# An attention and mixture-of-experts kernel: three buffers for x, and the last pair's first two groups stored later

## The chip, the cores and the metric

One core of one Trainium2 chip runs the whole program. The number that counts is the device time of one execution in microseconds (us); the median of three executions stands for the kernel. Lower is better.

The engines are named as in the profile: PE (TensorE, matmuls), DVE (VectorE), ACT (ScalarE), POOL (GpSimd) and SP (SyncE, which here does nothing but issue transfers and read expert numbers). Each works through its own list of instructions in order. The lists meet at semaphores.

## The reference

Windowed attention on 8 batches, 8 heads, 576 positions, 64 channels; half of the heads see the last 32 positions, half see every fourth of the last 128. Its output, as 4608 rows of 512, goes through a mixture of experts with 4 groups of 4 experts: each row picks a group, then an expert in the group, and gets that expert's two-layer result times the two probabilities.

```python
scores = np.where(mask, scale * q @ k.T, -1e9)
x = softmax(scores) @ v                       # 4608 rows of 512
g_idx = argmax(x @ w_group); e_idx = argmax(x @ w_expert[g_idx])
h  = np.maximum(x[rows] @ w1[g, e], 0.0)
out[rows] = g_w * e_w * (h @ w2[g, e])
```

## The kernel before

**Attention.** The program runs 36 steps (`NT`), `NJ` = 9 to a pair of batches; a step covers 64 positions of both batches of the pair. Three steps make a group `g` (12 groups), the unit of the transfers: q, k and v are loaded by group, and the output x of three steps lies in one tile `xg[g]`, which has two buffers (line 369). The loop over `s` (line 950) is skewed: in turn `s` it computes the scores of step `s`, transposes the probabilities of step `s-1`, multiplies step `s-2` with v (`av`), writes its x (`normalise`, line 371, on DVE) and transposes the x of step `s-3`.

**Stores of x.** `store_x(g, bbs)` writes the rows of one batch (`bbs` = 0 or 1) of a group to the table `xd` in DRAM, in four or five transfers of the SP queue (lines 346, 351 and 358). They are issued in `normalise`: batch 0 when the third step of the group is written, batch 1 one turn later. Group 11, the last, is stored behind the loop (line 1009). The last pair is groups 9, 10 and 11. A tile x of group `g` may be written again only when the stores of the group before in the same buffer have landed.

**Routing.** When a pair is through, `route` computes which expert each of its rows goes to, in small pieces between the steps (`slot`). One of its pieces builds, on POOL, a mask `okm` (line 510) and from it two halves of the table `mv` (line 513); PE multiplies both with `ohl` into `tb_ps` (line 553), from which DVE updates the table of rows per expert (lines 562 to 567). The probabilities go to `xd` too (`gt`, line 547).

**The experts that start early.** After the second and the third pair the two fullest experts so far are picked (`pick`), their first rows are fetched from `xd` (`fetch_rows`, on POOL, tile `xe`), and their feed-forward work (`early`) runs among the last steps of attention and behind it, in the order that the string `TAIL` spells. Then come all other experts, one after the other, up to the end.

**Weights.** `load_weights` brings an expert's weights in 8 chunks (0 to 7) of 512 KB (line 645, SP queue), through four staging buffers `w`. ACT writes the high half of a chunk as float16 (line 667); the low half, the chunk less its high half, is made by DVE (line 663) or, for the chunks in `ASIDE`, by POOL in two instructions (line 660 scales the chunk in place, line 661 subtracts). For the first early expert these are all chunks but chunk 6. A staging buffer is free for the chunk four further on when its low half is done. The first expert's chunks are spread over turns 27 and on, one a turn (`prefetch`, `WSTEPS`, line 1003).

**Who sets the order.** PE's and DVE's lists are in the order of the code in this part of the program (line 949), so are SP's and ACT's (line 141). POOL's list is arranged by the scheduler that builds the program, which means that a change of the code elsewhere can rearrange it. Within a list nothing overtakes. An SP transfer also waits until the one eight places before it has landed.

Of the kernel before, what the change touches and what calls it, by code (L numbers as in the profile page):

```python
# [8 lines left out]
F32 = mybir.dt.float32  # L9
F16 = mybir.dt.float16  # L10
BF16 = mybir.dt.bfloat16
I32 = mybir.dt.int32
# [5 lines left out]
P = 128  # L18
# [5 lines left out]
NE = 16  # L24
NBP = B // 2
NJ = S // 64
NT = NBP * NJ
# [12 lines left out]
MAXOV = 64  # L40
# [4 lines left out]
EARLY_STEPS = {NT - 1: 1, NT: 2, NT + 1: 1}  # L45
TAIL = "ararrrarrawrrrawrwarrrrrrwbwarbrrrwbrrrrwbrrrwbTwbbb"
ASIDE = ((0, 1, 2, 3, 4, 5, 7), (4, 5, 6))
NR = NE + NEARLY
REG = 8192
NCHK = NTOK // P  # L50
# [6 lines left out]
def moe_attention_kernel(ctx, tc, q, k, k0, v, cmask, wgate, wpack, out):  # L57
    nc = tc.nc
    pool = lambda name, bufs=1, **kw: ctx.enter_context(tc.tile_pool(name=name, bufs=bufs, **kw))
    cp = pool("cp")  # L60
# [130 lines left out]
        nc.vector.memset(capt[:, r : r + 1], float(CAPS[r]))  # L191
    top = cp.tile([P, NEARLY, NE], F32, name="top")
    topc = cp.tile([P, NEARLY], F32, name="topc")
    perm = cp.tile([P, NE, NE], F32, name="perm")
    ordf = cp.tile([P, NE], F32, name="ordf")
    ordi = cp.tile([P, NE], I32, name="ordi")
    ovn = cp.tile([P, 1], I32, name="ovn")
    ovt = cp.tile([P, MAXOV, 2], I32, name="ovt")
    E16 = [cp.tile([P, TPB + 1, 4, 4], BF16, name=f"E16{i}") for i in range(2)]
    for t in E16:  # L200
        nc.vector.memset(t, 0.0)
# [15 lines left out]
    ap = apool("ap", 3)  # L217

    def run(gens, n=1):
        got = None  # L220
        for _ in range(n):
            while gens:
                try:
                    got = next(gens[0])
                    break
                except StopIteration:
                    gens.pop(0)
            else:
                return None
        return got  # L230
# [107 lines left out]
    xg = {}  # L338

    def store_x(g, bbs):  # L340
        bp, k = g // 3, g % 3
        for bb in bbs:
            row = (2 * bp + bb) * S
            xv = xg[g].rearrange("p j (h c) -> p j h c", h=2)
            own = xd[row + 192 * k : row + 192 * k + 192, :].rearrange("(j i) d -> i j d", i=64)
            nc.sync.dma_start(own[:, :, 0:256], xv[64 * bb : 64 * bb + 64, :, 0])
            for i0, i1, j0, j1, t0 in class_runs(k):
                for_all = xd[row : row + S, 256:512].rearrange("(t r) d -> r t d", r=4)[t0 % 4]
                first, n = t0 // 4, i1 - i0
                if j1 - j0 == 1:  # L350
                    nc.sync.dma_start(for_all[first : first + n], xv[64 * bb + i0 : 64 * bb + i1, j0, 1])
                    continue
                at = bass.AP(
                    for_all.tensor,
                    for_all.offset + first * 4 * XW,
                    [[4 * XW, n], [256 * XW, j1 - j0], [1, 256]],
                )
                nc.sync.dma_start(at, xv[64 * bb + i0 : 64 * bb + i1, j0:j1, 1])

    def normalise(n):  # L360
        o = oo.pop(n)
        ov = o[:, :, 0:260].rearrange("p k (s c) -> p k s c", c=65)
        den = ap.tile([P, 2, 4], F32, name="den")
        nc.vector.tensor_scalar_add(den, ov[:, :, :, 64], 1e-9 / SX)
        slot()
        nc.vector.reciprocal(den, den)
        slot()
        if n % 3 == 0:
            xg[n // 3] = ap.tile([P, 3, 512], F32, name="x", bufs=2)
        x = xg[n // 3][:, n % 3]  # L370
        nc.vector.tensor_tensor(
            x.rearrange("p (k s c) -> p k s c", k=2, s=4),
            ov[:, :, :, 0:64],
            den.unsqueeze(3).broadcast_to([P, 2, 4, 64]),
            ALU.mult,
        )
        if n % 3 == 2:
            if n < NT - 1:
                store_x(n // 3, (0,))
        elif n % 3 == 0 and n:  # L380
            store_x(n // 3 - 1, (1,))
        st[n] = x.rearrange("p (s w c) -> p s w c", s=4, w=2)

# [222 lines left out]
    def order():  # L606
        T = lambda nm, shape, dt=F32: sm.tile([P] + shape, dt, name=nm)
        key = T("key", [NE])
        nc.vector.tensor_tensor(key, base[NBP], base[0], ALU.subtract)
        for r in range(NEARLY):  # L610
            nc.vector.scalar_tensor_tensor(
                key, top[:, r], float((NEARLY - r) * NTOK), key, ALU.mult, ALU.add
            )
        nc.vector.scalar_tensor_tensor(key, key, float(NE), iota[:, 0:NE], ALU.mult, ALU.subtract)
        sq = T("sq", [NE, NE])
        nc.vector.tensor_tensor(
            sq,
            key.unsqueeze(1).broadcast_to([P, NE, NE]),
            key.unsqueeze(2).broadcast_to([P, NE, NE]),
            ALU.is_gt,  # L620
        )
        rank = T("rank", [NE])
        nc.vector.tensor_reduce(rank, sq, axis=AX.X, op=ALU.add)
        nc.vector.tensor_tensor(
            perm,
            rank.unsqueeze(1).broadcast_to([P, NE, NE]),
            iota[:, 0:NE].unsqueeze(2).broadcast_to([P, NE, NE]),
            ALU.is_equal,
        )
        nc.vector.tensor_tensor(sq, perm, iota[:, 0:NE].unsqueeze(1).broadcast_to([P, NE, NE]), ALU.mult)  # L630
        nc.vector.tensor_reduce(ordf, sq, axis=AX.X, op=ALU.add)
        nc.vector.tensor_copy(ordi[:, NEARLY:NE], ordf[:, NEARLY:NE])
# [282 lines left out]
    def prefetch():  # L915
        for r in range(NEARLY):
            while r not in ev:
                yield
            todo.extend(load_weights(ev[r], wsets[r], lambda i: i in ASIDE[r], 2 - 2 * r))
            todo.pop(0)()  # L920
# [29 lines left out]
    for s in range(NT + 3):  # L950
        ripe = bool(gate)
        if s < NT:
            scores(s)
        if s % 3 == 2 and s // 3 + 2 < NT // 3:
            load_k(s // 3 + 2, (0,))
        if s % 3 == 0 and 2 <= s // 3 + 1 < NT // 3:
            load_k(s // 3 + 1, (1,))
        if s % 3 == 1 and 1 <= s // 3 + 1 < NT // 3:
            carry_k(s // 3 + 1)
        if s % 3 == 0 and NQ <= s // 3 + 2 < NG:  # L960
            load_q(s // 3 + 2) if s // 3 + 2 < NG - 1 else None
        if s // 3 + 2 == NG - 1:
            load_q(NG - 1, s % 3, s % 3 + 1)
        if 0 <= s - 2 < NT:
            av(s - 2)
            if ripe:
                gate.clear()
        if start:
            n = start[0]
            routes.append(route(n, turned_logits(n)))  # L970
            rate[0] = RATE[n]
        if 0 <= s - 1 < NT:
            transpose_p(s - 1)
        if s < NT:
            softexp(s)
        if s == 0:
            nc.vector.memset(flat(vt[2]), 0.0)
        if 0 <= s - 3 < NT:
            transpose_x(s - 3)
        if s % 3 == 1 and 2 <= s // 3 + 2 < NG - 1:  # L980
            load_v(s // 3 + 2)
        if s // 3 + 1 == NG - 1 and s % 3 < 2:
            load_v(NG - 1, ((0, 2), (2, 3))[s % 3])
        if 0 <= s - 2 < NT:
            normalise(s - 2)
        if start:
            n = start.pop()
        if gate == [3]:
            gate.clear()
        slot()  # L990
        if s % 3 == 0 and s // 3 + 1 < NT // 3:
            shift_v(s // 3 + 1, 0, 2)
        if s % 3 == 1 and s // 3 + 1 < NT // 3:
            shift_v(s // 3 + 1, 2, 3)
        for r in picked:
            if r not in ev:
                expert(r)
        if s == min(WSTEPS):
            wq.append(prefetch())
        if s == NT - 1:  # L1000
            eb.append(early(0, new_x(fe, EARLY[0]), fe, EARLY[0]))
        run(eb, EARLY_STEPS.get(s, 0))
        run(wq, WSTEPS.get(s, 1))
        if s >= 3 and (s - 3) % NJ == NJ - 1:
            bp = (s - 3) // NJ
            if bp < NBP - 1:
                start.append(bp)
        run(eq)
# [6 lines left out]
    fh = pool("fh", 2, reuse_waits="tile")  # L1015
    rows = pool("rows", 2, reuse_waits="tile")
    fs = pool("fs", 3, reuse_waits="tile")
    wB[:] = [fs.tile([P, 4096], F16, name=nm, bufs=1) for nm in ("wb1h", "wb1l", "wb2h", "wb2l")]
    big = pool("big", reuse_waits="tile")
    stages.append(pool("wst2", reuse_waits="tile"))  # L1020

    def overflow():
# [16 lines left out]
        )  # L1039
        num = T("num", [NR])  # L1040
        nc.vector.tensor_reduce(num[:, 0:NE], cg, axis=AX.X, op=ALU.add)
# [4 lines left out]
        yield  # L1046
        cum = T("cum", [NR])
        nc.vector.tensor_copy(cum, num)
        for r in range(1, NR):
            nc.vector.tensor_tensor(cum[:, r : r + 1], cum[:, r : r + 1], cum[:, r - 1 : r], ALU.add)  # L1050
            if r % 4 == 0:
                yield
        nc.vector.tensor_copy(ovn, cum[:, NR - 1 : NR])
        lo = T("lo", [NR])
        nc.vector.tensor_tensor(lo, cum, num, ALU.subtract)
        ex = T("ex", [NR])
        nc.vector.tensor_copy(ex[:, 0:NE], ordf)
# [60 lines left out]
    run(wq, 100)  # L1118
    cur = begin(0)
    order()  # L1120
    expert(2)
    run(e1, 100)
# [128 lines left out]
```

## Time and profile before

| | |
|---|---|
| median of 3 executions | 559.17 us (558.96 to 560.13) |
| the profiled execution | 565.16 us |
| its span, first to last instruction | 563.4 us |
| PE busy | 537.1 us, 95% of the span |
| DVE, ACT, POOL busy | 369.9, 316.3, 241.1 us |
| transfers | 134.31 MB, mean 238 GB/s |

Times in the rows count from the start of the profiled span. The last scores are issued at 136.3 us, so attention takes about the first quarter and the experts the rest. The engine whose busy share matters most is PE; a busy PE counts matmuls that overlap, so its 95% says that there are few gaps, not that each matmul runs at its best.

### The profile page before, as it was taken

To read this page: it belongs to the slowest core of one execution; us is meant where nothing else is said; L and a number is where in the kernel's file an instruction comes from. 1 tells how busy PE (TensorE), PEld (TensorE's weight loads), DVE (VectorE), ACT (ScalarE), POOL (GpSimd) and SP (SyncE) were. 2 spreads that over 40 slices of the span, in tenths; PEclk is the share of its full clock that TensorE was granted. 3 is DMA by queue.
4 is the path that set the end of the run, shared out by engine and by line. 5 is a ranking of instruction groups with operands and counts; after the bars stand their busy time and mean duration, and the time that the engine had idled before them with its cause. 6 is when DMAs were issued, how large, how long until landed. Compare 5 with 4: busy or idle time off the path is not lost. (4 is left out here: it accounts for less than half of the span.)

```text
span 563.4 us, 16475 instructions
## 1 busy us (share of the span) xinstructions
PE 537.1 (95%) x6577; PEld 384.8 (68%) x6577; DVE 369.9 (66%) x842; ACT 316.3 (56%) x563; POOL 241.1 (43%) x219
## 2 busy tenths in 40 slices
PE   6899999998898999999999999999999999999995
PEld 4777878786765765657666667575656756787883
DVE  8776786877787226574859597755647477658640
ACT  6555556567663335564646565564646567647741
POOL 6796566758958232603041513224160531221212
PEclk9999999999999999999999999999999999999999
DMA  8988988798592716978787786979697699898841
GB/s 284 407 288 278 320 268 279 233 317 290 162 305 55 259 41 127 335 180 258 185 286 165 271 211 226 255 225 293 175 315 199 217 295 276 293 333 229 257 113 30
DMA packets 79265, 134.31 MB, mean 238 GB/s; under 512 B 42988, under 2 KB 52630, under 8 KB 79186
## 3 DMA queue, kind: packets, MB, share of 16 engines
q1 hardware_dynamic: 72258, 113.65, 66.5%
q0 software_dynamic: 6784, 19.51, 10.4%
q8 instruction: 53, 0.87, 0.6%
q14 instruction: 26, 0.21, 0.1%
q10 hardware_dynamic: 144, 0.07, 0.0%
HBM read 106.16 MB, written 19.29 MB: 223 GB/s over the span
## 5 line engine op out<-in xcount | busy, mean ns | idle before, releaser
L818 POOL DMA_INDIRECT out<-yr,sent x31 | 38.4, 1238 | 220.0 <-ACT yr L817 202.0
L762 DVE SCALAR_TENSOR_TENSOR hl<-a,hh 128x256 f16<-128x256 f32 (+13 forms) x144 | 60.7, 424 | 97.6 <-ACT hh L761 77.4
L754 PE MATMUL a<-xs,wb1h 128*128 128x256 f16 (+7 forms) x576 | 97.9, 275 | 2.6 <-DVE hl L762 2.5
L754 PE MATMUL a<-xs,wa 128*128 128x304 f16 (+7 forms) x864 | 97.5, 272 | 1.5 <-issue 0.8
L761 ACT ACTIVATE hh<-a 128x256 f16<-128x256 f32 (+13 forms) x144 | 55.4, 388 | 72.1 <-PE a L754 55.3
L754 PEld LDWEIGHTS <-wa 128*128 128x128 f16 x864 | 79.0, 98 | 19.0 <-issue 2.5
L847 PEld LDWEIGHTS <-hh 128*128 128x128 f16 x480 | 46.9, 98 | 54.7 <-issue 1.2
L663 DVE SCALAR_TENSOR_TENSOR wa<-w,wa 128x1024 f16<-128x1024 f32 x57 | 69.1, 1230 | 18.5 <-ACT wa L667 14.6
L754 PE MATMUL a<-xs,wb1l 128*128 128x256 f16 (+7 forms) x288 | 78.3, 275 | 0.0
L847 PE MATMUL y<-wa,hh 128*128 128x512 f16 x240 | 73.9, 379 | 0.5 <-issue 0.5
L667 ACT ACTIVATE wa<-w 128x1024 f16<-128x1024 f32 x64 | 66.9, 1055 | 11.3 <-DMA w<-wpack 8.8
L754 PEld LDWEIGHTS <-wb1h 128*128 128x128 f16 x576 | 55.0, 98 | 15.6 <-issue 3.4
L817 ACT ACTIVATE yr<-y,cs 128x512 f32<-128x512 f32 (+3 forms) x31 | 21.3, 687 | 56.1 <-issue 26.4
L693 POOL DMA_INDIRECT xr<-xd,sent x41 | 42.1, 1026 | 19.2 <-issue 11.0
L847 PE MATMUL y<-wb2h,hh 128*128 128x512 f16 x120 | 45.6, 380 | 0.0
L847 PE MATMUL y<-wb2h,hl 128*128 128x512 f16 x120 | 45.5, 379 | 0.0
L847 PE MATMUL y<-wb2l,hh 128*128 128x512 f16 x120 | 45.5, 379 | 0.0
L847 PE MATMUL y<-wa,hl 128*128 128x512 f16 x120 | 45.5, 379 | 0.0
L663 DVE SCALAR_TENSOR_TENSOR wb2l<-w,wb2h 128x1024 f16<-128x1024 f32 x29 | 36.3, 1281 | 13.7 <-ACT wb2h L667 13.7
L304 ACT COPY pt<-t 128x512 f32<-128x512 f32 x36 | 21.0, 584 | 37.8 <-PE t L303 37.7
L315 PE MATMUL o<-vs,pt 128*32 128x130 f32 x576 | 39.9, 273 | 2.3 <-DVE own L498 0.9
L283 DVE TENSOR_REDUCE mx<-s 128x8 f32<-128x512 f32 x36 | 24.7, 687 | 24.5 <-PE s L273 24.4
(207 smaller groups left out, 1088.2 us busy)
## 6 DMA issues: line engine op xcount, KB each, us to landing
w<-wpack SPq DMA_DIRECT2D x128, 512.0 KB
kb<-k SPq DMA_DIRECT2D x24, 384.0 KB
vt<-v SPq DMA_DIRECT2D x14, 390.0 KB
qb<-q SPq DMA_DIRECT2D x7, 768.0 KB
xd<-x SPq DMA_DIRECT2D x24, 192.0 KB
wa<-v SPq DMA_DIRECT2D x6, 390.0 KB
wa<-q SPq DMA_DIRECT2D x3, 768.0 KB
xd<-x SPq DMA_DIRECT2D x32, 48.0 KB
```

What stands on the lines that cost most here:

```text
L283: nc.vector.tensor_reduce(mx, s, axis=AX.X, op=ALU.max)
L304: nc.scalar.copy(pt[n % NPT], t)
L315: nc.tensor.matmul(o[32 * j : 32 * j + 32, c // 2, at : at + 130], pt[n % NPT][:, c, 32 * j : 32 * j + 32], t[:, :, jl, bb * 4 + c, :], st ...
L663: nc.vector.scalar_tensor_tensor(l, w32, SW, h, ALU.mult, ALU.subtract)
L667: nc.scalar.mul(parts(i)[0], w32s[i], SW)
L693: nc.gpsimd.indirect_dma_start(out=xr[0:n], out_offset=None, in_=xd[0:known, :], in_offset=bass.IndirectOffsetOnAxis(ap=ent[0:n, t : t + 1 ...
L754: nc.tensor.matmul(a[:, 0:cap], ww[:, c * FF + f * P : c * FF + f * P + P], xx[:, c, 0:cap], start=(i == 0), stop=(i == len(mm) - 1),)
L761: nc.scalar.activation(hh[:, f, 0:cap], a[:, 0:cap], AF.Relu)
L762: nc.vector.scalar_tensor_tensor(hl[:, f, 0:cap], a[:, 0:cap], 0.0, hh[:, f, 0:cap], ALU.max, ALU.subtract)
L817: nc.scalar.activation(yr[0:n, :], yp[0:n, :], AF.Copy, scale=cs[0:n, t : t + 1])
L818: ins = nc.gpsimd.indirect_dma_start(out=out, out_offset=bass.IndirectOffsetOnAxis(ap=ent[0:n, t : t + 1], axis=0), in_=yr[0:n, :], in_off ...
L847: nc.tensor.matmul(yp, h[:, f, t * P : t * P + n], ww[:, f * DM : f * DM + DM], start=(i == 0), stop=(i == len(mm) - 1),)
```

## The change

The tile x gets three buffers. `normalise` still issues the stores of groups 0 to 8 (`LATER` is 9); those of groups 9 and 10 are issued by the loop, behind the weight chunk of the turn: group 9, both batches, in turn 34, group 10's batches in turns 35 and 36. Group 11 stays behind the loop. Three tiles of `order` and `overflow` (`sq`, `perm`, `ovt`) move into a pool that is made after attention.

```diff
+LATER = NT // 3 - 3
+STORES = {NT - 2: (0, (0, 1)), NT - 1: (1, (0,)), NT: (1, (1,))}
...
-    perm = cp.tile([P, NE, NE], F32, name="perm")
-    ovt = cp.tile([P, MAXOV, 2], I32, name="ovt")
...
-            xg[n // 3] = ap.tile([P, 3, 512], F32, name="x", bufs=2)
+            xg[n // 3] = ap.tile([P, 3, 512], F32, name="x", bufs=3)
...
         if n % 3 == 2:
-            if n < NT - 1:
+            if n // 3 < LATER:
                 store_x(n // 3, (0,))
-        elif n % 3 == 0 and n:
+        elif n % 3 == 0 and 0 < n // 3 <= LATER:
             store_x(n // 3 - 1, (1,))
...
-        sq = T("sq", [NE, NE])
+        sq = fs.tile([P, NE, NE], F32, name="sqo", bufs=1)
...
         run(wq, WSTEPS.get(s, 1))
+        if s in STORES:
+            store_x(LATER + STORES[s][0], STORES[s][1])
...
+    perm = fs.tile([P, NE, NE], F32, name="perm", bufs=1)
+    ovt = fs.tile([P, MAXOV, 2], I32, name="ovt", bufs=1)
```

In SP's list, turns 31 to 34 begin in this way before: the stores of group 9 (the first four rows are batch 0, the four behind chunk 4 batch 1), with the weight chunks 4, 5 and 6 among them (`w_2524`, `w_2598`, `w_2678`).

```order
L346 DMA xd<-x 64x3x256
L358 DMA xd<-x 16x3x256
L358 DMA xd<-x 48x2x256
L351 DMA xd<-x 48x256
L645 ISA
L645 DMA w_2524<-wpack 128x1024
L346 DMA xd<-x 64x3x256
L358 DMA xd<-x 16x3x256
L358 DMA xd<-x 48x2x256
L351 DMA xd<-x 48x256
L645 ISA
L645 DMA w_2598<-wpack 128x1024
```

Now, behind the same loads of v, chunks 4 to 7 (`w_2518`, `w_2588`, `w_2668`, `w_2755`) and the reading of the second expert's number (line 913) stand first, and the first store of group 9 behind all of them.

```order
L645 ISA
L645 DMA w_2518<-wpack 128x1024
L645 ISA
L645 DMA w_2588<-wpack 128x1024
L645 ISA
L645 DMA w_2668<-wpack 128x1024
L913 TENSOR_LOAD ordi
L913 ISA x2
L645 ISA
L645 DMA w_2755<-wpack 128x1024
L346 DMA xd<-x 64x3x256
L358 DMA xd<-x 16x3x256
```

What moved: eighteen stores went behind chunk 7; of them thirteen now stand ahead of the store of `gt`, where eighteen stood before, and five behind it.

POOL's list from the low half of chunk 3 (`w_2441`) to the fetch of the second early expert's rows, before:

```order
L661 TENSOR_TENSOR wa_91<-w_2441,wa_91 128x1024
L510 TENSOR_TENSOR okm<-okm,mine_214 128x72
L513 TENSOR_TENSOR mv<-E_208,okm 128x576
L660 TENSOR_SCALAR w_2524<-w_2524 128x1024
L513 TENSOR_TENSOR mv<-E_208,okm 128x576
L661 TENSOR_TENSOR wa_92<-w_2524,wa_92 128x1024
L660 TENSOR_SCALAR w_2598<-w_2598 128x1024
L661 TENSOR_TENSOR wa_92<-w_2598,wa_92 128x1024
L660 TENSOR_SCALAR w_2770<-w_2770 128x1024
L661 TENSOR_TENSOR wa_92<-w_2770,wa_92 128x1024
L693 DMA xe_224<-xd,ente_231 128x528
```

And the same stretch now, where `w_2439` is chunk 3, `w_2518` and `w_2588` are chunks 4 and 5, and `w_2755` is chunk 7:

```order
L661 TENSOR_TENSOR wa_91<-w_2439,wa_91 128x1024
L660 TENSOR_SCALAR w_2518<-w_2518 128x1024
L661 TENSOR_TENSOR wa_92<-w_2518,wa_92 128x1024
L660 TENSOR_SCALAR w_2588<-w_2588 128x1024
L661 TENSOR_TENSOR wa_92<-w_2588,wa_92 128x1024
L510 TENSOR_TENSOR okm<-okm,mine_212 128x72
L513 TENSOR_TENSOR mv<-E_206,okm 128x576 x2
L660 TENSOR_SCALAR w_2755<-w_2755 128x1024
L661 TENSOR_TENSOR wa_92<-w_2755,wa_92 128x1024
L693 DMA xe_222<-xd,ente_229 128x528
```

What moved: the low halves of chunks 4 and 5, four instructions, went ahead of `okm` and both halves of `mv`. PE's list has the same instructions in the same order as before.

## Rows read from the trace of the kernel before

**Rows 1.** Windows: busy us of each engine, PE's clock, transfers.
```profile
185.00:540.00 355.00, 352.55 (x3166) 239.11 (x3165) 227.13 (x433) 202.41 (x332) 103.22 (x95) 1.00 0.80 237
```

**Rows 2.** Timeline of PE: start, us, instruction, [idle before <- releaser].
```profile
141.19 0.66 PE L729 MATMUL pt<-id,xe 128*128 128x128 f32 x4 [0.34 <-ACT pt L304]
...
147.66 0.47 PE L553 MATMUL tb_ps<-mv,ohl 128*64 128x64 f16 x18
148.07 0.84 PE L754 MATMUL a<-xs,wa 128*128 128x128 f16 x12
149.80 0.63 PE L393 MATMUL tx<-id,x 128*128 128x128 f32 x4 [0.89 <-DVE own L562]
...
161.71 0.66 PE L729 MATMUL pt<-id,xe 128*128 128x128 f32 x4 [0.33 <-DMA xe<-xd,ente]
...
176.38 0.38 PE L754 MATMUL a<-xs,wb1h 128*128 128x256 f16 x2 [1.72 <-DVE hl L762]
```

**Rows 3.** Timeline of SP's queue: start, us to issue, transfer.
```profile
131.19 0.36 SPq L645 DMA_DIRECT2D w<-wpack  x1
...
141.94 0.37 SPq L645 DMA_DIRECT2D w<-wpack  x1
...
145.97 0.38 SPq L547 DMA_DIRECT2D xd<-gt  x1
```

**Rows 4.** Timeline of POOL.
```profile
138.45 1.06 POOL L660 TENSOR_SCALAR w<-w 128x1024 f32<-128x1024 f32 x1
...
141.69 0.31 POOL L510 TENSOR_TENSOR okm<-okm,mine 128x72 f32<-128x72 f32 x1
142.08 1.18 POOL L513 TENSOR_TENSOR mv<-E,okm 128x576 f16<-128x576 bf16 x1
143.23 1.04 POOL L660 TENSOR_SCALAR w<-w 128x1024 f32<-128x1024 f32 x1
144.25 1.18 POOL L513 TENSOR_TENSOR mv<-E,okm 128x576 f16<-128x576 bf16 x1
145.38 2.15 POOL L661 TENSOR_TENSOR wa<-w,wa 128x1024 f16<-128x1024 f32 x1
147.50 2.01 POOL L660 TENSOR_SCALAR w<-w 128x1024 f32<-128x1024 f32 x1
...
155.11 1.08 POOL L693 DMA_INDIRECT xe<-xd,ente  x1 [0.15 <-DVE mx L434]
```

**Rows 5.** Timeline of ACT, high halves of chunks 4 and 5.
```profile
136.18 1.06 ACT L667 ACTIVATE wa<-w 128x1024 f16<-128x1024 f32 x1 [0.98 <-DMA w<-wpack]
...
139.60 1.06 ACT L667 ACTIVATE wa<-w 128x1024 f16<-128x1024 f32 x1 [0.54 <-POOL w L660]
```

**Rows 6.** Timeline of DVE.
```profile
141.14 0.69 DVE L371 TENSOR_TENSOR x<-o,den 128x512 f32<-128x512 f32 x1 [0.17 <-DMA xd<-x]
...
146.68 1.94 DVE L663 SCALAR_TENSOR_TENSOR wa<-w,wa 128x1024 f16<-128x1024 f32 x1
...
148.96 0.69 DVE L371 TENSOR_TENSOR x<-o,den 128x512 f32<-128x512 f32 x1
...
173.06 2.94 DVE L663 SCALAR_TENSOR_TENSOR wb2l<-w,wb2h 128x1024 f16<-128x1024 f32 x1
```

**Rows 7.** Costliest groups: busy us, mean ns of one, idle before.
```profile
L663 DVE SCALAR_TENSOR_TENSOR wa<-w,wa 128x1024 f16<-128x1024 f32 x57 | 69.1, 1230 | 18.5 <-ACT wa L667 14.6
```

**Rows 8.** PE's timeline at its start, then windows behind its last matmul.
```profile
4.17 0.59 PE L254 MATMUL s<-masks,idb 128*128 128x512 bf16 x1 [4.17 <-DMA masks<-cmask]
...
6.15 1.93 PE L273 MATMUL s<-wa,qb 128*32 128x128 f32 x32
...
10.92 1.08 PE L273 MATMUL s<-kb,qb 128*32 128x128 f32 x32
...
557.70:561.80 4.10, 0.00 (x0) 0.00 (x0) 0.00 (x0) 0.69 (x1) 1.02 (x1) 1.00 0.18 68
561.90:563.40 1.50, 0.00 (x0) 0.00 (x0) 0.00 (x0) 0.00 (x0) 0.00 (x0) 0.50 0.00 0
```

## The prediction

> **What bounds the kernel now.** I read the windows first. From 185 us to 540 us, where the experts run one behind the other, PE is busy 352.55 of 355 us at a granted clock of 1.00 [rows 1]. Nothing there can be gained by an earlier transfer, and what PE loses before 185 us it can't win back there: a delay at 150 us arrives at the end in full. So the question is what the change does to PE between about 130 us, where SP's list first differs (chunk 4, issued at 131.19 [rows 3], now comes ahead of the stores), and 185 us.
>
> Then I read PE's timeline of that stretch for its waits. None of them is for a weight chunk or for a store of x. The waits that bear on the change are short: 0.34 us at 141.19 behind ACT's `pt`, 0.89 at 149.80, 0.33 at 161.71 for the fetched rows `xe`, and 1.72 at 176.38 for DVE's `hl` [rows 2]. The wait at 149.80 is labelled with a DVE instruction of line 498 to 562; the one that ended it is the write of x that began at 148.96 and took 0.69, up to 149.65 [rows 6]. (A releaser is inferred; the tile that `tx` turns is x.)
>
> Third, POOL's timeline, because it is the one list that the build has rearranged. From 138.45 to 155.1 us POOL has no gap: each instruction starts when the one before it ends [rows 4]. POOL is off PE's path there only because the two halves of `mv` are done at 143.26 and 145.43 (starts 142.08 and 144.25, 1.18 each) and PE asks for them at 147.66, without any idle time ahead of it [rows 2, 4]. That is a cover of 2.2 us.
>
> **The change part by part.**
>
> *Three buffers for x.* The one wait that goes is DVE's 0.17 us at 141.14 for a store of x [rows 6]. PE's next work hangs on that x, so at most 0.17 us.
>
> *Weights issued earlier.* Chunk 4 was issued at 131.19, behind half of group 9's stores, and ACT waited 0.98 us for it at 136.18 [rows 3, 5]. Now it is issued directly behind the loads of v, more than 2 us earlier, and that wait goes; so does ACT's 0.54 at 139.60. PE profits by its 0.34 at 141.19, which hangs on ACT. Together PE is at most 0.5 us earlier at `tb_ps`. These 0.5 us would be the whole gain of the change; they count only if PE finds `mv` ready.
>
> *POOL's list.* It is the term that decides. Up to the end of chunk 3's low half, at 141.69, nothing on POOL changes: chunks 2 and 3 and the loads of v are issued before the first moved store. There POOL used to make `okm` and `mv`. Now the low halves of chunks 4 and 5 come first. Are they ready? ACT had finished their high halves at 136.18 + 1.06 = 137.24 and 139.60 + 1.06 = 140.66 already with the later issue [rows 5]. So POOL starts them at once, and pays for each what chunk 3 cost from its start to the next instruction's: 141.69 - 138.45 = 3.24 us [rows 4]. Two make 6.48, up to 148.17. Then `okm` and the first half of `mv` (143.23 - 141.69 = 1.54) and the second half (1.18): 150.89 us.
>
> Between them stands a meeting with DVE. The row at 147.50 shows POOL's scaling at 2.01 us where its neighbours take 1.04 to 1.06, and it overlaps DVE's low half of chunk 6, which at 146.68 took 1.94 where the mean of its group is 1.230 [rows 4, 6, 7]. In turn that one had begun while POOL was in its subtraction of 145.38. In the new order POOL is in chunk 5's subtraction at 146.68 (from about 146.0 to 148.17), so the same meeting happens, and `okm` loses what the scaling lost, 2.01 - 1.05 = 0.96. With it the second half of `mv` ends at 151.85. Bounds: 0, if the two miss each other, and 2.94 - 1.23 = 1.7, what the worst such meeting in the rows cost the DVE side [rows 6, 7]; I take 0.96, since it is the same pair.
>
> [...]
>
> PE can't start `tb_ps` before both halves are there (its first two matmuls wait for one each), and what is behind it in PE's list, the next piece of `early` (0.84) and `tx`, can't pass. So `tb_ps` starts at 151.85 in place of 147.66: +4.19. That PE arrives there up to 0.5 us earlier only makes the stall longer.
>
> *What is given back.* The wait of 0.89 at 149.80 goes: `tx` is now reached at about 151.85 + 0.41 + 0.84 = 153.1, and its x, even if the meeting makes DVE 0.96 later, is there by 150.6. The wait of 0.33 at 161.71 may go as well: POOL's fetch stood at 155.11, and now comes behind chunk 7's low half at 151.85 + 3.24 = 155.1, practically where it was, while PE comes 3.3 us later. But what PE does behind it needs DVE's halves, which move with PE, so I count nothing for it; bounds 0 and 0.33.
>
> *The stores themselves.* SP reaches them behind chunk 7, whose staging buffer is only free when chunk 3's low half is done, at 141.7; its issue at 141.94 stays [rows 3, 4]. Then 13 stores, and behind them `gt` of the third pair, for which the fetch waits. Between chunk 7 and `gt` lay five stores: at most (145.97 - 141.94 - 0.37) / 5 = 0.73 us each [rows 3]. So `gt` is issued at 151.8 at the latest, in place of 145.97. A landing bounded by chunk 4's (issued 131.19, used 136.18: 5.0 us) makes 156.8, 1.7 us behind the fetch's turn; rows that came 161.71 - 155.11 = 6.6 us after their fetch began then are there at 163.4, and PE is there at 161.71 - 0.33 + 3.3 = 164.7 [rows 2, 3, 4]. Hidden, with 1.3 us to spare. The other five stores, the second expert's chunks and group 11 come later by some 5 us at most; the second expert's matmuls stand in PE's list behind the `xe` of 161.71 [rows 2], ten us further on, so I count nothing; if that cover is too short, PE waits for what is missing of it. The three moved tiles change no instruction's place on PE; I cost them at nothing.
>
> *Sum.* +4.19 - 0.89 = +3.3 us. The profiled execution took 565.16 us (span 563.4 and 1.8 around it), 6.0 above the median of 559.17; a stall inside the program adds the same to either. So 568.5 with the profiler and 559.17 + 3.3 = **562.5** without, 0.6% slower. What one measurement of this kernel can tell from no change is about 0.2%, 1.1 us.
>
> **The rivals.**
>
> *PE's clock falls in the stall: 564.9.* PE would be idle for 4.2 us, up to 4.7 if it arrives early. [...] At the start of the program, after 4.17 us of idling, 32 score matmuls took 1.93 us at 6.15 and 1.08 at 10.92, so PE was slow from 4.17 to somewhere between 8.1 and 10.9 us: 3.9 to 6.7 us in which 1 - 1.08 / 1.93 = 0.44 is lost, 1.7 to 3.0 us. In the middle, +2.4. [...]
>
> [...]
>
> *The delay is partly won back before 185 us: 560.8.* The wait of 1.72 at 176.38 is for an `hl` that stands behind a DVE low half of 2.94 us, a meeting with POOL again [rows 2, 6]. If the shift parts the two, that instruction takes 1.23 and PE gains 1.7: +1.6 is left. For it speaks that meetings of this kind depend on tenths; against it that DVE, ACT and POOL there all wait for one another and move together.
>
> *Nothing is lost, or it is a little faster: 558.7.* That is the change without the POOL term: the 0.5 us of the earlier weights. It holds if the second half of `mv` is done by 147.7. From 141.69 there are 6.0 us; 2.7 go to `okm` and `mv`, and 3.3 are left for work that took 6.48. POOL would have to be at chunk 3 over 3 us earlier, and the rows show no gap in which it could be. The profile's POOL spans are called rough, so I don't give it nothing.
>
> *The stall is there and all of it is hidden: 559.2.* It needs waits of 3.3 us behind 150 that would fall away; the rows show 0.33 and 1.72.
>
> **How the numbers follow.** My forecast 66%, the clock 15%, partly won back 10%, hidden 5%, faster 4%. The forecast's own range is 561.2 (no meeting, 0.33 won) to 563.2 (a worse meeting). The range for 8 in 10 takes in the case partly won back and most of the clock: 560.5 to 565.3. Faster by over 0.2%: 5%; within: 7%; slower: 88%.
>
> **What would show it.** PE's `tb_ps` that stood at 147.66 has an idle time of 3 to 4.7 us, put down to POOL's `mv`; the wait of 0.89 behind it is gone; POOL's `okm` starts at 148 to 149 us; chunks 4 to 6 are issued by 134 us and the first store of group 9 behind 142; PE in the windows behind 185 us is as full as before. I am wrong if `tb_ps` has no idle time before it, if POOL's low halves there take far less than 3.24 us a chunk, or if PE's idle time between 165 and 185 us shrinks by more than 1 us.

## The result, and the profile after

| | us |
|---|---|
| changed kernel, median of 6 executions | 562.49 (561.86 to 565.62) |
| kernel before, median of 6 on the same chip | 559.65 (558.92 to 560.52) |
| ratio | 1.0062, 95% interval 1.0036 to 1.0089 |
| ratio, measured again (first experiment) | 1.0070, 1.0041 to 1.0099 |

The change makes the kernel 0.6 to 0.7% slower, 3.5 to 3.9 us; 562.5 was predicted. Single executions of one kernel lie up to 8 us apart, and up to 11 with those of a slower state that no ratio uses, so below the ratios count, and a profile tells which wait is there, not what the kernel costs.

From 185 us on nothing was lost. The windows of the changed kernel, in answer to [rows 1]:

```profile
185.00:540.00 355.00, 355.00 (x3190) 241.45 (x3189) 229.81 (x441) 203.88 (x332) 102.42 (x98) 1.00 0.80 238
```

PE is busier than in [rows 1] by 2.45 us; that is a peculiarity of the trace of before, since with the stores unmoved (`e1_buffers` below) it is 354.85.

POOL's timeline of the changed kernel, in answer to [rows 4], has the order and the sum of the forecast; only the meeting with DVE falls on `mv` (3.18 us for both halves, 2 x 1.18 in [rows 4]) and not on `okm`:

```profile
142.24 1.05 POOL L660 TENSOR_SCALAR w<-w 128x1024 f32<-128x1024 f32 x1
143.37 2.15 POOL L661 TENSOR_TENSOR wa<-w,wa 128x1024 f16<-128x1024 f32 x1
145.48 1.05 POOL L660 TENSOR_SCALAR w<-w 128x1024 f32<-128x1024 f32 x1
146.62 2.14 POOL L661 TENSOR_TENSOR wa<-w,wa 128x1024 f16<-128x1024 f32 x1
148.72 0.31 POOL L510 TENSOR_TENSOR okm<-okm,mine 128x72 f32<-128x72 f32 x1
149.11 3.18 POOL L513 TENSOR_TENSOR mv<-E,okm 128x576 f16<-128x576 bf16 x2
```

From the end of chunk 3's low half to the end of `mv` it takes 152.29 - 142.24 = 10.05 us; the prediction had 151.85 - 141.69 = 10.16. PE's timeline of the same execution, those of its waits that bear on this, in answer to [rows 2]:

```profile
130.19 1.70 PE L273 MATMUL s<-kb,qb 128*32 128x128 f32 x32 [2.11 <-DMA kb<-k]
...
151.20 0.19 PE L553 MATMUL tb_ps<-mv,ohl 128*64 128x64 f16 x1 [1.42 <-POOL mv L513]
152.34 0.45 PE L553 MATMUL tb_ps<-mv,ohl 128*64 128x64 f16 x17 [0.95 <-POOL mv L513]
...
164.63 0.66 PE L729 MATMUL pt<-id,xe 128*128 128x128 f32 x4 [0.48 <-DMA xe<-xd,ente]
165.84 0.66 PE L729 MATMUL pt<-id,xe 128*128 128x128 f32 x4 [0.55 <-DMA xe<-xd,ente]
```

`tb_ps` now waits 1.42 + 0.95 = 2.4 us for POOL's `mv`, and the 0.89 at `tx` is gone. Two things were not forecast. PE waits 0.48 + 0.55 us for `xe`, the fetched rows, where before it was 0.33. And SP is behind: its timeline, in answer to [rows 3]:

```profile
130.25 12.38 SPq L645 DMA_DIRECT2D w<-wpack  x4
142.74 0.65 SPq L346 DMA_DIRECT2D xd<-x  x1
143.44 1.23 SPq L358 DMA_DIRECT2D xd<-x  x2
...
151.04 0.38 SPq L547 DMA_DIRECT2D xd<-gt  x1
...
154.41 2.14 SPq L645 DMA_DIRECT2D w<-wpack  x4
```

Each transfer of a store holds SP for about 0.6 us here: eighteen of them and `gt` take 154.41 - 142.74 = 11.67 us, 0.61 each. The last row is the second expert's first four chunks. In the kernel before they went out one by one, the first of them 7.5 us ahead of the fetch; that row was not shown ahead, and is this one:

```profile
147.56 7.76 SPq L645 DMA_DIRECT2D w<-wpack  x4
```

Now all four leave within 2.1 us, at the moment at which POOL fetches `xe` (156.27 in the changed kernel). What that is worth is the subject of the second half of the experiments.

### The profile page after: what moved, and what is told of

Same layout as the page of the kernel before. It is cut to its first block, busy times and chain, and to the rows that moved or that the text cites. A ratio compares the mean times of both kernels' runs of the same rounds, so it can differ in the third digit from the quotient of the medians.

```text
span 563.9 us, 16473 instructions
## 1 busy us (share of the span) xinstructions
PE 535.3 (95%) x6577; PEld 386.2 (68%) x6577; DVE 370.4 (66%) x842; ACT 316.7 (56%) x563; POOL 236.9 (42%) x219
## 5 line engine op out<-in xcount | busy, mean ns | idle before, releaser
L818 POOL DMA_INDIRECT out<-yr,sent x31 | 34.3, 1107 | 219.5 <-ACT yr L817 203.0
L663 DVE SCALAR_TENSOR_TENSOR wb2l<-w,wb2h 128x1024 f16<-128x1024 f32 x29 | 36.2, 1272 | 16.6 <-ACT wb2h L667 15.0
```

Source lines behind the costliest of these rows:

```text
L663: nc.vector.scalar_tensor_tensor(l, w32, SW, h, ALU.mult, ALU.subtract)
L818: ins = nc.gpsimd.indirect_dma_start(out=out, out_offset=bass.IndirectOffsetOnAxis(ap=ent[0:n, t : t + 1], axis=0), in_=yr[0:n, :], in_off ...
```

## The experiments

**The changed kernel again, and its first part alone.** `e0_after_again` is the changed kernel, unedited. `e1_buffers` keeps three buffers and the moved tiles and leaves the stores where they were:

```diff
-LATER = NT // 3 - 3
-STORES = {NT - 2: (0, (0, 1)), NT - 1: (1, (0,)), NT: (1, (1,))}
+LATER = NT // 3 - 1
+STORES = {}
```

Expected of the first: 

> The changed kernel once more, on the same chip as the three that follow, so that they can be held against it. All theories: 562.5 us against 559.6 of before (ratio 1.005). Its profile tells whether the wait of 2.1 us for kb at 130 us and the half clock behind it, seen in the first profile of the changed kernel, belong to the kernel or to that one execution. POOL theory: tb_ps idles 3.5 to 4.5 us if kb is waited for 1.6 us as before, and less by what PE is late if kb comes later.

Expected of the second: 

> One part alone: x has three buffers and the three tiles are moved, the stores stay where they were; every list is as before. POOL theory: as before, 559.5 us, since the only wait that goes is DVE's 0.17 us. Rival that the third buffer or the moved tiles cost something by themselves: 562.5.

Measured: 1.0070 (1.0041 to 1.0099) and 1.0021 (0.9992 to 1.0050). The second interval holds no change, though a loss of up to 0.5% as well, and there was no wait at `tb_ps`: most of the loss, at least, is in the moved stores. In the profile of the changed kernel run again PE comes to `tb_ps` as early as POOL's forecast assumed, and waits longer; for `xe` it does not wait at all:

```profile
146.88 0.19 PE L553 MATMUL tb_ps<-mv,ohl 128*64 128x64 f16 x1 [2.42 <-POOL mv L513]
148.02 0.45 PE L553 MATMUL tb_ps<-mv,ohl 128*64 128x64 f16 x17 [0.95 <-POOL mv L513]
...
161.11 1.04 PE L729 MATMUL pt<-id,xe 128*128 128x128 f32 x8
```

Behind the wait at `tb_ps` the clock falls. Windows of that execution, the granted clock is the third number from the end:

```profile
146.00:148.80 2.80, 0.97 (x26) 0.84 (x25) 0.70 (x3) 0.00 (x0) 2.80 (x3) 1.00 0.70 142
148.80:152.20 3.40, 3.40 (x36) 3.14 (x36) 3.16 (x7) 1.45 (x4) 2.57 (x3) 0.51 0.70 143
152.20:155.00 2.80, 2.80 (x58) 2.41 (x51) 0.06 (x1) 0.64 (x2) 1.83 (x2) 0.99 0.98 369
```

For 3.4 us PE is busy at a granted clock of 0.51, a loss of up to 3.4 x 0.49 = 1.7 us. In the first profile the clock had fallen behind the wait of 2.11 at 130.19 instead (0.50 from 130.50 to 133.90; 32 score matmuls in 1.70 us where [rows 8] has 1.08), and not at `tb_ps` (1.00 from 151.20 to 153.30).

**POOL's order alone, put in and taken out.** `e3_before_mv_late` is the kernel before with `okm` and `mv` kept behind chunk 5's low half on POOL; no transfer moves. `e2_mv_first` is the changed kernel with the low halves of chunks 4 and 5 kept behind `mv` (`behind(a, b)` puts `a` behind `b` in POOL's list):

```diff
...
+    behind(table[0][0], lows[5][1])    # e3, in the kernel before
...
+    behind(lows[4][0], table[0][1])    # e2, in the changed kernel
+    behind(lows[5][0], table[0][1])
```

Expected of the first: 

> The kernel before with nothing changed but POOL's list: okm and mv are held behind the low half of chunk 5, as the build of the changed kernel has them; stores, buffers and all other lists are as before. POOL theory: 562.4 to 563.0 us (+3.3), with 3.5 to 4.5 us of idle time at tb_ps. Rival that the stores do it: 559.6, as before.

Expected of the second: 

> The change with POOL's list put right: the low halves of chunks 4 and 5 are held behind both halves of mv, nothing else differs from the changed kernel. POOL theory: the whole loss goes, 558.7 to 559.6 us, and tb_ps has no idle time before it. Rival that the later stores or the earlier weight loads themselves cost the time (crowding the loads of k, or gt late): it stays at 562 to 562.5.

Measured: 1.0043 (1.0017 to 1.0068) and 1.0049 (1.0019 to 1.0079). POOL's order by itself does cost, about 0.4% where 0.6% was expected, with the wait at the forecast place in the profile of the first, 2.59 us where 3.5 to 4.5 was expected:

```profile
150.11 0.19 PE L561 MATMUL tb_ps<-mv,ohl 128*64 128x64 f16 x1 [1.64 <-POOL mv L519]
151.25 0.64 PE L561 MATMUL tb_ps<-mv,ohl 128*64 128x64 f16 x17 [0.95 <-POOL mv L519]
```

In this profile PE wins part of it back further on: its waits for `hl` between 165 and 185 us are 0.23 and 0.58, where before they were 0.57, 0.17 and 1.72. But to take POOL's order out of the changed kernel did not win it back: my expectation for the second missed. Its profile has no wait at `tb_ps` and two others:

```profile
150.91 0.88 PE L397 MATMUL tx<-id,x 128*128 128x128 f32 x4 [2.02 <-DVE own L570]
...
165.35 0.66 PE L739 MATMUL pt<-id,xe 128*128 128x128 f32 x4 [1.79 <-DMA xe<-xd,ente]
```

The first is of this edit's own making: POOL's two subtractions now stood side by side, and DVE's low half of chunk 6 took 3.06 us beside them (1.94 in [rows 6]), so the x behind it was late; and behind that wait the granted clock was 0.52 from 151 to 154 us, where it had been 1.00 from 148 to 151. The second is not.

**One chunk instead of two.** `e4_before_mv_one_late` puts `okm` and `mv` behind chunk 4 alone, in the kernel before.

```diff
...
+    behind(table[0][0], lows[4][1])
+    behind(lows[5][0], table[0][1])
```

Expected: 

> The kernel before with one difference in POOL's list: okm and both halves of mv stand behind the low half of chunk 4 alone (behind those of chunks 4 and 5 the same edit cost 0.43%). POOL theory, in which only what reaches past PE's turn at tb_ps counts: 141.69 + 3.24 + 2.72 = 147.65 us, just when PE comes, so a wait at tb_ps of 0 to 0.5 us and a ratio of 0.9995 to 1.001. Rival, in which each displaced chunk costs its own 3.24 us (half of the effect of two): ratio 1.002 to 1.003.

Measured: 1.0015 (0.9980 to 1.0050), and no wait at `tb_ps` in the profile. The wait agrees with the theory that the first chunk is covered; the interval is too wide to exclude the rival.

**POOL's list exactly as before, in the changed kernel.** `e6_after_old_pool` restores the interleaving of [rows 4], so that against the kernel before only SP's list and the buffers differ.

```diff
...
+    behind(lows[4][0], table[0][1])
+    behind(table[0][2], lows[4][0])
+    behind(lows[4][1], table[0][2])
+    behind(lows[5][0], lows[4][1])
+    behind(lows[6][0], lows[5][1])
```

Expected: 

> The changed kernel with POOL's list in exactly the order of the kernel before (okm, first half of mv, scaling of chunk 4, second half of mv, subtraction of chunk 4, chunk 5), so that only the stores and the weights differ from before. Theory 1, POOL's order is the whole loss and the last try failed because it put the two subtractions of chunks 4 and 5 side by side, against which DVE's low half of chunk 6 took 3.06 us: that instruction goes back to about 1.9 us, no wait over 1 us between 145 and 152, ratio 0.998 to 1.001. Theory 2, the block of 13 stores costs something of its own, since SP issues the four chunks of the second expert only behind it, at about 154 instead of 147.6, and the fetch of xe then shares the transfer engines with them: tb_ps without a wait, xe lands 7 to 9 us behind its issue instead of 5, PE waits 1 to 2 us for it near 165, ratio 1.002 to 1.004.

Measured: 1.0064 (1.0030 to 1.0098), no less than the changed kernel. DVE's low half was back at 2.06 us and `tb_ps` did not wait. PE's waits in its profile:

```profile
148.54 0.63 PE L397 MATMUL tx<-id,x 128*128 128x128 f32 x4 [1.01 <-DVE own L572]
...
160.91 0.66 PE L741 MATMUL pt<-id,xe 128*128 128x128 f32 x4 [1.60 <-DMA xe<-xd,ente]
163.14 0.66 PE L741 MATMUL pt<-id,xe 128*128 128x128 f32 x4 [1.57 <-DMA xe<-xd,ente]
```

3.17 us for `xe`. POOL issued the fetch at 153.86, as early as ever; it landed later. The view of the tile `xe` gives its time from issue to landing:

```profile
DMA to landing us min/median/max: 7.9/7.9/7.9
```

Where the first of the second expert's first four chunks starts 7 to 8 us ahead of the fetch and the others follow one by one, the median of the known landings is 5.0 (stores unmoved), 5.1 (POOL's order alone) and 5.1 (one chunk). Where all four go out within 2 to 4 us, starting some 1.3 us ahead of it, it is 7.9 (the changed kernel again), 7.6 (`e2_mv_first`) and 7.9. Theory 1, POOL alone, has fallen.

**The chunks ahead of the stores.** `e10_stores_behind_weights`, on top of the last kernel:

```diff
-STORES = {NT - 2: (0, (0, 1)), NT - 1: (1, (0,)), NT: (1, (1,))}
+STORES = {NT + 1: (0, (0, 1)), NT + 2: (1, (0, 1))}
```

Expected: 

> As the run with POOL's old order, but the 16 transfers of groups 9 and 10 are issued behind the probabilities gt of the third pair and behind the first four chunks of the second expert. Theory 2 (the block of stores ahead of these chunks costs 1 to 2 us): the four chunks are issued from about 147 us again, xe lands about 5 us behind its issue, PE doesn't wait for it, and the ratio is 0.001 to 0.004 below that of the run with POOL's old order. Theory 1 (POOL alone): no difference between the two beyond 0.001. A third possibility: the next four chunks, which now stand behind 26 stores where 8 stood, come late, and PE waits for one of them behind 170 us; then it is slower, 1.002 to 1.006.

Measured: 1.0148 (1.0099 to 1.0197), the third possibility, and worse than the 1.002 to 1.006 given for it. (Groups 9 and 10 have eighteen transfers, not the 16 of the expectation.) The fetch is well again: issued at 153.29, it lands after 5.2 us, though the 26 transfers of the stores of groups 9 to 11 begin at 153.55 beside it. But the next four chunks are issued at 169.72 instead of 160.20, and PE pays for that:

```profile
176.00 0.58 PE L766 MATMUL a<-xs,wb1h 128*128 128x256 f16 x2 [9.89 <-DVE hl L774]
```

So it is not the stores' own traffic that slows the fetch, but the chunks that they push; and any chunk behind them is pushed. (The granted clock was 1.00 from 165.40 to 168.90 and 0.50 from 169.00 to 176.00, within this wait; behind it the matmuls with `wb1l` took 0.42 us up to 178.94 and 0.27 from 179.43 on.)

**The chunks late, no store moved.** `e15_before_late_chunks` is the kernel before with group 11's eight stores ahead of the second expert's first four chunks; nothing else in any list differs. `e16_before_both` adds the POOL order of `e3_before_mv_late`.

```diff
...
-WSTEPS = {NT - 9: 1, NT + 1: 2, NT + 2: 0}
+WSTEPS = {NT - 9: 1, NT + 1: 1, NT + 2: 0}
...
     store_x(NG - 1, (0, 1))
+    run(wq, 1)
...
```

Expected of the first: 

> The kernel before with one difference in SP's list: the first four chunks of the second expert are issued behind the eight stores of group 11 instead of ahead of them. No other store moves, POOL's list stays, x has two buffers. Theory 2 (what the block of stores costs in the changed kernel is that it pushes these four chunks, 2 MB, up to the fetch of xe, which then lands 7.6 to 7.9 us behind its issue instead of 5.0 to 5.2): the chunks are issued at about 154 to 157, xe lands 7 to 8 us behind its issue, PE waits 2 to 3.5 us for it, no wait at tb_ps, ratio 1.003 to 1.006. Rival, that it is the moved stores themselves that slow the fetch or the waits before it: xe lands after 5 to 5.5 us, ratio 0.999 to 1.0015.

Expected of the second: 

> The kernel before with both single faults and none of the moved stores: okm and mv behind the low halves of chunks 4 and 5 on POOL (alone: 1.0043), and the second expert's four chunks behind the stores of group 11. Theory 2 with overlap (PE that comes late at tb_ps also comes late for xe, so the two delays cover one another): a wait of 2 to 3 us at tb_ps, one of 0 to 1.5 us for xe, ratio 1.004 to 1.0075, about that of the changed kernel (1.0062 and 1.007). Rival, the two add: ratio 1.008 to 1.010.

Measured: 1.0104 (1.0065 to 1.0143), more than expected, and 1.0082 (1.0050 to 1.0114); the medians are the same, 563.5 against 558.9 us. In the first the chunks leave from 154.01 on, between the two fetches of `xe` at 153.03 and 154.41: the one ahead of them lands after 4.0 us, the one behind their first after 6.6. PE's waits:

```profile
161.05 0.66 PE L741 MATMUL pt<-id,xe 128*128 128x128 f32 x4 [1.00 <-DMA xe<-xd,ente]
165.17 0.27 PE L766 MATMUL a<-xs,wb1h 128*128 128x256 f16 x1 [0.87 <-ACT xs L742]
167.10 0.27 PE L766 MATMUL a<-xs,wb1h 128*128 128x256 f16 x1 [1.67 <-DVE xs L743]
```

1.00 is for `xe`, and 2.54 for `xs`, its float16 halves. These 2.54 are not the fetch's doing. PE had transposed all of `xe` at 161.05 + 0.66 = 161.71; but in ACT's list the cast to `xs` stands behind the high halves of the four late chunks, and in DVE's behind a low half:

```profile
163.10 1.06 ACT L679 ACTIVATE wb1h<-w 128x1024 f16<-128x1024 f32 x1 [0.20 <-DMA w<-wpack]
164.06 1.05 ACT L742 CAST xs<-pt 128x512 f16<-128x512 f32 x2
...
164.52 1.22 DVE L675 SCALAR_TENSOR_TENSOR wb1l<-w,wb1h 128x1024 f16<-128x1024 f32 x1
...
165.71 0.68 DVE L743 TENSOR_TENSOR xs<-pt,xs 128x512 f16<-128x512 f32 x1
```

And behind these waits the granted clock is 0.50, as the window shows:

```profile
167.80:171.20 3.40, 3.40 (x19) 2.27 (x16) 2.38 (x7) 1.33 (x2) 3.22 (x3) 0.50 0.72 231
```

Up to 1.7 us of what this run costs beyond the expectation is the clock's. With both faults `tb_ps` waits 2.95 + 0.95 us, and for `xe` PE doesn't wait at all, although it takes 7.4 us to land. By its number alone this run would suit the rival, whose 1.008 to 1.010 was reckoned with less for the chunks. Against what was measured it doesn't: 0.43% and 1.04% alone would make 1.47%, and the interval ends at 1.14% (by the medians 0.60% and 0.81% alone, 0.81% together). One delay covers much of the other.

**Group 10's stores behind the chunks.** `e14_group10_behind_weights`: POOL as before, group 9's eight transfers where the change has them, group 10's ten behind the chunks.

```diff
-STORES = {NT - 2: (0, (0, 1)), NT - 1: (1, (0,)), NT: (1, (1,))}
+STORES = {NT - 2: (0, (0, 1)), NT + 2: (1, (0, 1))}
```

Expected: 

> The changed kernel with both taken back and the earlier weights kept: POOL's list as before, and of the 13 stores ahead of gt only the eight of group 9 stay there; group 10's ten are issued behind the second expert's first four chunks. If POOL's order and the late burst are all that the change costs: no wait at tb_ps, xe lands 5 to 6 us behind its issue and PE waits 0 to 0.7 us for it, ratio 0.998 to 1.0015, unless the next four chunks, now behind 18 stores instead of 8, come late for hl (with 26 stores PE waited 9.9 us there); the chunks would be issued at about 164 instead of 160, as in the run with POOL's old order, where PE's waits for hl were 2.7 us in all, so I expect none. If a third cause is at work, 1.003 or more.

Measured: 1.0129 (1.0081 to 1.0177). `xe` lands after 5.0 us and PE waits 0.39 for it, but the next four chunks leave at 167.59 instead of the 164 that I had counted, and PE pays for that:

```profile
174.20 0.38 PE L766 MATMUL a<-xs,wb1h 128*128 128x256 f16 x2 [4.88 <-DVE hl L774]
```

My reckoning that 18 stores ahead of them would fit took the 164 from the run with POOL's old order, and compared two executions that stand 2.9 us apart (`tb_ps` starts at 149.21 here, at 146.28 there). Counted from `tb_ps` the chunks leave after 18.4 us here and 17.5 there, only 0.9 later. What the reckoning missed is that in that run PE stood at `xe` for 3.17 us and so came too late to wait long for them: the delay at `xe` was covering this one.

**The stores left out.** `e17_stores_left_out`, on top of POOL's old order:

```diff
-STORES = {NT - 2: (0, (0, 1)), NT - 1: (1, (0,)), NT: (1, (1,))}
+STORES = {}
...
+        if s == 14:
+            nc.sync.dma_start(
+                xd[NTOK - 9 * P : NTOK, 0:256].rearrange("(t p) c -> p t c", p=P),
+                xe[0][0][:, 0:256].unsqueeze(1).broadcast_to([P, 9, 256]),
+            )
...
```

(`xe[0][0]` holds zeros then; the second transfer writes the other 256 columns.)

Expected: 

> The changed kernel with POOL's old order and without the stores of groups 9 and 10: they are left out (16 instructions of the list), so two thirds of the last pair's rows reach the experts as zeros, written in turn 14 by two transfers of 1.2 MB each, at a place where PE's idle time is small in every run so far. Everything else, the earlier weights too, stays. If all that the moved stores cost is SP's time at this place (about 0.6 us for each store, ahead of the second expert's chunks), then SP issues these chunks from about 147 us, xe lands about 5 us behind its issue, the next four are issued at about 160, and PE waits no more than before: ratio 0.996 to 1.000, the earlier weights bringing at most 0.5 us. If three buffers, the moved tiles or the earlier weights themselves cost something, the ratio is 1.002 or more. If the two transfers of zeros disturb the loads around 60 to 70 us, a new wait shows there and is to be taken off.

Measured: 1.0105 (1.0069 to 1.0142), and by its total it settles nothing, since the zeros did disturb the loads around them. PE's longest wait from 60 to 100 us is 4.76, where the kernel before has 0.5:

```profile
77.38 1.93 PE L277 MATMUL s<-kb,qb 128*32 128x128 f32 x32 [4.76 <-issue]
```

With the slow matmuls behind it (1.93 instead of 1.08 us) that is 5.6 us, of 5.9 by the ratio and 7.5 by the medians. In the stretch in question the profile is that of the kernel before: `xe` lands after 4.8 us, the next four chunks leave at 166.74 in an execution that stands 6.2 us later (`tb_ps` at 153.87 against 147.66), and PE's waits behind the one for k, up to the last for `hl`, make 5.7 us (0.86, 0.29, 0.60, 1.00, 0.35, 0.49, 0.63, 1.50), against 6.2 before and 9.1 with the stores and POOL's old order. Subtracting like this is weaker than a run; it speaks against a third cause and doesn't exclude one. The table at the end of this section does it without subtracting.

**The same edit where PE does wait for a load.** `e13_group8_later`: the kernel before with three buffers, and one batch of group 8 stored behind the loads of group 11's k and v (on top of `e1_buffers`, POOL's list as before).

```diff
-        elif n % 3 == 0 and 0 < n // 3 <= LATER:
+        elif n % 3 == 0 and 0 < n // 3 <= LATER and n // 3 != 9:
...
-STORES = {}
+STORES = {NT - 5: (-3, (1,))}
```

Expected: 

> The kernel before with three buffers for x and one batch of stores moved: batch 1 of group 8 is issued behind the loads of k and v of group 11 instead of ahead of them; POOL's list is that of before. It is the same kind of edit at a place where PE does wait for the load: 1.55 us for k at 129.61. Theory (an earlier load is worth what PE waits for it, if no other list is disturbed): that wait goes, PE is 1.0 to 1.5 us earlier at tb_ps and at the end; ratio 0.997 to 0.999. Rival: something else ends last there, a wait of 1 us or more appears before 150 us, ratio 0.9995 to 1.002.

Measured: 1.0015 (0.9978 to 1.0051): the rival's wait is there, while the interval excludes neither. The wait for k is gone (1.55 in the trace of before, 1.24 in `e1_buffers`), and PE waits for ACT's `pt` instead, 2.12 us where the same wait was 0.34 in before and 1.45 in `e1_buffers`:

```profile
142.62 0.66 PE L741 MATMUL pt<-id,xe 128*128 128x128 f32 x4 [2.12 <-ACT pt L308]
```

No version beat the kernel before.

**One stretch in all profiles.** In these profiles most of what sets single executions apart lies ahead of the change or far behind it. So take PE's time from its first `rk_ps` of the last pair (line 470 in before and in the changed kernel) to the first `y` that the second expert makes of `wb2h` (line 847 there). Times in us:

| kernel | `rk_ps` starts | `y<-wb2h` starts | between |
|---|---|---|---|
| before | 132.44 | 179.00 | 46.56 |
| `e1_buffers`, stores unmoved | 129.17 | 175.55 | 46.38 |
| `e4_before_mv_one_late` | 131.10 | 177.10 | 46.00 |
| `e3_before_mv_late`, POOL's order alone | 133.31 | 180.34 | 47.03 |
| changed kernel | 134.63 | 183.29 | 48.66 |
| changed kernel again | 129.28 | 178.73 | 49.45 |
| `e6_after_old_pool` | 131.21 | 180.40 | 49.19 |
| `e17_stores_left_out`, POOL's old order | 138.80 | 184.35 | 45.55 |
| `e15_before_late_chunks` | 130.62 | 181.03 | 50.41 |
| `e16_before_both` | 131.02 | 180.94 | 49.92 |

The changed kernel loses 2.1 to 3.5 us here against the three without either fault. With POOL's old order it is 3.6 us longer with the moved stores than without them, and without them no longer than before: one profile each, but nothing is left for a third cause in this stretch. POOL's order alone shows as 0.5 to 1.0 us only, less than its ratio says.

## Why the prediction was right, and where it was not

- **Buffers and tiles cost nothing, DVE's 0.17 goes:** no clear difference with the buffers alone (1.0021, interval over 1; 46.38 us in the stretch above, where before has 46.56).
- **Weights earlier, PE at most 0.5 us earlier at `tb_ps`:** chunks 4 to 7 are issued from 130.25 on. ACT's waits for chunks 4 and 5 [rows 5] are gone as forecast; its wait for chunk 3 grew, from 0.64 to 1.72 us, in both profiles of the changed kernel. PE does gain: from the start of `rk_ps` to its arrival at `tb_ps` it takes 15.1 to 15.2 us in all seven profiles with early weights, and 15.2, 15.7, 16.3 and 16.6 with the stores unmoved (before, `e4_before_mv_one_late`, `e1_buffers`, `e15_before_late_chunks`). The trace that the 0.5 was read from is the shortest of the four, so the gain was more than it showed, up to 1.5 us. It was lost again behind `tb_ps`: no run with early weights was faster.
- **POOL, +4.19 at `tb_ps`:** the mechanism is shown, by the wait in two profiles of the changed kernel and by the order alone in the kernel before (0.43%, 2.4 us). From chunk 3's end to the second `mv` 10.16 us were forecast; 10.05 and, in the changed kernel run again, 10.16 were measured, with the meeting where it was put in the latter: `okm` took 1.29 instead of 0.31 us beside DVE's low half of chunk 6 (143.40, 2.00 us). In the other profile `mv` pays nearly the same price, 3.18 us in place of 2 x 1.18, beside that low half (148.73, 1.38). PE's wait was 2.4 and 3.4 us, less than the term: in the first profile PE came late itself (2.11 for k, then a clock of 0.50), in the second POOL had begun chunk 3 about 0.7 us earlier against PE than in the trace of before.
- **Given back, 0.89 at `tx`:** gone in both profiles.
- **The clock, a rival at 15%:** it did fall behind `tb_ps` in one of the two profiles, for 3.4 us (0.51 from 148.80 to 152.20), and in `e3_before_mv_late` likewise (0.50 from 151.10 to 154.50), though not behind every wait, as the last section lists. The sum left it out, and a stall shorter than forecast made up for it: 3.4 - 0.89 + 1.7 = 4.2 us in one execution, against 3.3 predicted and 3.5 to 3.9 measured.
- **Partly won back before 185 us, a rival at 10%:** not in the changed kernel, whose waits for `hl` make 3.0 and 2.6 us in its two profiles (2.46 before); with POOL's order alone they shrink to 0.81.
- **The step that failed: "The stores themselves", "Hidden, with 1.3 us to spare".** It assumed that rows fetched at the same time come at the same time, 6.6 us after the fetch. It looked for the cost of late chunks at PE's matmuls with them, ten us further on, and counted nothing. The chunks come 6.9 us later (154.41 against 147.56; 4.7 and 6.2 counted from `rk_ps` in the two profiles, where "some 5 us at most" was forecast), and they hurt at two places ahead of those matmuls. One is the fetch beside which they now run: 7.6 to 7.9 us to landing in place of 5.0 to 5.1. The other is ACT and DVE, which have to split these chunks before they get to `xs`: 2.54 us of PE's waits in `e15_before_late_chunks`, against 1.00 for the fetch. In the changed kernel the two end together: ACT is through with the fourth chunk at 165.57 + 1.06, after a wait of 2.52 for it, when PE has just transposed `xe` (165.84 + 0.66), so its profile can't tell what either would cost alone. The fetch stands in a queue of its own: from 150 to 160 us in `e15_before_late_chunks` `software_dynamic` moved 0.53 MB (two fetches of 128 x 528 float32 make 0.54), and `hardware_dynamic`, with the chunks and stores, 2.05 MB. How the chunks slow it is not shown by any run.

So the number was right, its account half of the truth, and that the two meet at 562.5 is luck. In the changed kernel there are two delays, each of which alone costs two thirds of the whole or more: POOL's `mv` (0.43% alone) and the late chunks (0.64% with POOL's old order; 1.04% in the kernel before). PE, late at `tb_ps`, is late at `xe` too, and waits 1.03 us there in one profile and not at all in the other, instead of 3.17. That is why the sum with POOL alone came out right, and why undoing POOL's order won nothing. The late chunks are shown as a cause by `e15_before_late_chunks`; that the slower fetch is their only way, or the larger one, is not shown. That the two delays explain all of the 3.5 to 3.9 us is argued: every kernel that undid both brought in a third delay elsewhere, and the stretch above, where nothing is left over, holds 2.1 to 3.5 us of it in one profile each.

## What to carry to other kernels

A transfer that is moved out of the way of an early one is in the way of a later one: count SP's time for all of it (0.6 us a store here) against what stands behind it, up to the next place where the queue waits anyway, and ask beside which transfers these will then run, and what stands behind their users in the lists of the other engines. When undoing a suspected cause brings nothing back, the cause is not refuted; look for a second delay that it had been covering, and put each alone into the kernel before. Where a scheduler arranges one engine's list, compare that list first.

## What had not been expected of the hardware

- The fetch of the second expert's rows, issued by POOL, landed after 7.4 to 7.9 us (medians of the changed kernel again, `e2_mv_first`, `e6_after_old_pool` and `e16_before_both`; single ones 6.3 to 8.8) where the 2 MB of that expert's first four chunks were issued around it, within 2 to 4 us in the first three. In `e15_before_late_chunks`, with the chunks starting between the two fetches, it was 4.0 and 6.6. Elsewhere it was 4.8 to 5.8, and 5.2 with the transfers of 26 stores beside it (`e10_stores_behind_weights`). The first early expert's fetch, issued at 119.02 in the changed kernel beside other loads, took 5.6.
- The granted clock fell behind waits of 2.11 us (0.50 from 130.50 to 133.90, changed kernel), of 2.42 + 0.95 (0.51 from 148.80 to 152.20, changed kernel again), of 2.02 (0.52 from 151 to 154, `e2_mv_first`), of 1.64 + 0.95 (0.50 from 151.10 to 154.50, `e3_before_mv_late`), of 0.87 and 1.67 (0.50 from 167.80 to 171.20, `e15_before_late_chunks`) and of 2.95 + 0.95 (0.50 from 149.80 to 156.60, `e16_before_both`). It did not fall behind one of 3.36 (1.00 from 128.40 to 131.80, with POOL's old order) or of 2.12 (`e13_group8_later`, whose mean over the whole span is 0.999, as in before): in these profiles the wait's length alone doesn't tell.
